# A RetNet attention block with an MLP behind it: how two token blocks start while weights arrive, and how two head pairs share the first batch

## The chip, the cores and the metric

One core of a Trainium2 chip. The metric is the device time of one execution in microseconds (us); the span is the time from the first to the last instruction in a profiled execution, about 2 to 3 us less. TensorE is called PE in the profile, VectorE DVE, ScalarE ACT, GpSimd POOL, SyncE SP.

## The reference, cut to what matters

```python
# q, k, v: (8 batches, 8 heads, 576 tokens, 64); float32
scores = (1/sqrt(64)) * q @ k^T
gamma  = 1 - 2**(-5 - h)                    # one per head
Dmat   = gamma**(i - j) where i >= j, else 0
attn   = (scores * Dmat) @ v
x      = attn as (4608 tokens, 512)
h      = x @ w_in                            # (512, 2048), float64 in memory
g      = max(h, 0) + alpha * min(h, 0)       # alpha: (2048,)
out    = g @ w_out                           # (2048, 512), float64 in memory
```

The weights and alpha are float64, so each 0.5 MB piece of weights is fetched raw and turned into float32 by three engines. The attention is done in chunks of 64 tokens: inside a chunk by scores, mask and values, between chunks by a running state, the scan. The 18 blocks of 256 tokens then go through the MLP. Most blocks use a scheme of seven products instead of eight, which needs sums and differences of weight blocks, the combinations.

## The kernel before: the parts concerned

The program works through 32 pairs of heads, four to a batch. Each pair runs transposes, scores, states with the scan, and values; between them stand units of the MLP and, at the start, weight pieces.

```python
def load_piece(src, dst):                       # one weight piece, 32 in all
    raw = raw_tile(at)
    nc.sync.dma_start(raw, src)
    lo, hi = raw[:, :, :, 0], raw[:, :, :, 1]
    nc.scalar.activation(a, hi.bitcast(FP32), ACTF.Abs)
    nc.scalar.activation(lo, lo.bitcast(UINT32), ACTF.Copy, scale=2.0 ** -29)
    nc.vector.tensor_scalar(a, a, HI_MIN, HI_MAX, ALU.max, ALU.min)        # the clamp
    c = ps_h.tile(...)                                                     # PSUM
    nc.vector.tensor_scalar(c, a.bitcast(INT32), 3, 0x3FFFFFF8, ...)       # the shift
    nc.vector.scalar_tensor_tensor(out=dst, in0=hi, scalar=-0x40000000, in1=c, ...)
    nc.gpsimd.tensor_tensor(out=dst, in0=dst, in1=lo, op=ALU.add)          # the last addition
# ... cut ...
def states(n, kn, vn):
    # ... 16 matmuls into ps ...
    nc.vector.tensor_copy(su[:, 0], ps[0][:, 0])
    for j in range(1, NJ - 1):                                             # the scan, 8 steps
        nc.vector.tensor_tensor(out=su[:, j], in0=ps[j % 2][:, j // 2], in1=su[:, j - 1], op=ALU.add)
    for h2 in range(2):
        nc.scalar.copy(sm[half(h2), :, h2], su[half(h2)])
# ... cut ...
for n, (b, c) in enumerate(pairs):
    if n + 1 < len(pairs):
        loaded[n + 1] = load_pair(n + 1)
    # ... cut ...
    kT, qT = transposes(n);            load_weights(2)
    at = scores(n, kT, qT);            load_weights(2)      # n < 8: four pieces a pair
    states(n, kn, vn)
    values(n, vn, qT, at)              # 18 matmuls with at, 16 with the running state
    # ... units of the MLP in between, cut ...
```

The profile counts two records for each of these float32 matmuls (32, 36 and 32 in its timelines), one for a transpose. All instructions stand in the in-order queue of their engine. Only block 0 uses plain products (eight), because its weights can't be combined before they have arrived.

## Time and profile before

| | before |
|---|---|
| time, median of 3 | 1097.5 us (1097.39 to 1097.9) |
| span of the profiled execution, mean granted TensorE clock | 1094.3 us, 0.978 |
| values of pairs 0, 1, 2, 3 end | 24.8, 38.4, 53.5, 68.5 us |
| TensorE without a pause from | 161.35 us |

The times of the values are read in TensorE's timeline: start plus duration of the last group of `pv<-qT,sums`, which follows the scan of the same pair. They are the milestones, since a batch's MLP units need the values of its four pairs.

```profile
22.16 2.61 PE L522 MATMUL pv<-qT,sums 128*64 128x64 f32 x32 [1.87 <-ACT sums L509]
36.18 2.17 PE L522 MATMUL pv<-qT,sums 128*64 128x64 f32 x32
51.35 2.17 PE L522 MATMUL pv<-qT,sums 128*64 128x64 f32 x32
66.34 2.17 PE L522 MATMUL pv<-qT,sums 128*64 128x64 f32 x32
```

Each pair follows the last by 14 to 15 us.

### The profile page before, as it was taken

The numbers are of one execution on the slowest core, as the hardware profiler recorded it, in microseconds if no ns is written. First come the engines' busy times: TensorE is split into PE (matmuls) and PEld (weight loads), VectorE is DVE, ScalarE is ACT, GpSimd is POOL, SyncE is SP. The second block draws the span as 40 slices with busy tenths as digits, with TensorE's granted clock in tenths as the row PEclk, the third lists the DMA queues.
The fourth block names the chain that finished last, engine by engine and source line by source line (L and its number), as shares of the span: only waits on it lengthen the run. The fifth ranks groups of instructions, "written<-read, shape, count | busy, mean of one in ns | idle before, by whom it ended". The sixth has DMA issues, their size and how long they took to land.

```text
span 1094.3 us, 25575 instructions
## 1 busy us (share of the span) xinstructions
PE 1052.2 (96%) x10465; PEld 940.9 (86%) x10465; DVE 777.3 (71%) x2160; ACT 162.8 (15%) x492; POOL 224.1 (20%) x264
## 2 busy tenths in 40 slices
PE   4769889999999999999999999999999999999998
PEld 3556668999999999999999999999999999999997
DVE  5577566776868776877676767687868676657665
ACT  3444431011001111101101111111111111000000
POOL 3888673110021102020012010210112000101000
PEclk9669999999999999999999999999999999999999
DMA  6746634121212222112121222222222010000000
GB/s 164 221 142 203 151 88 85 34 48 30 51 25 62 45 64 45 46 33 50 28 53 29 64 45 64 45 58 40 63 40 60 22 32 2 21 1 21 1 21 20
DMA packets 213205, 63.29 MB, mean 58 GB/s; under 512 B 202320, under 2 KB 202336, under 8 KB 213088
## 3 DMA queue, kind: packets, MB, share of 16 engines
q1 hardware_dynamic: 213088, 61.65, 23.9%
q8 instruction: 83, 1.36, 0.5%
q14 instruction: 34, 0.28, 0.1%
HBM read 52.17 MB, written 9.44 MB: 56 GB/s over the span
## 4 chain that ended last, share of the span: by engine, by line
PE 92%; DVE 3%; SPq 2%; ACT 1%; DMA 1%; issue 1%; POOL 0%; DVEq 0%; POOLq 0%; ACTq 0%
PE ph L376 40%; PE po L303 37%; PE pv L522 4%; PE ph L335 2%; PE pv L517 2%; PE ps L488 2%; PE po L318 2%; PE pu L500 2%; SPq L79 1%; DVE su L506 1%; SPq L81 1%; PE pt L461 1%; DVE wc L240 1%; DMA raw<-in_moe_w_in_dram 0%; DVE w_out L242 0%
## 5 line engine op out<-in xcount | busy, mean ns | idle before, releaser
L303 PE MATMUL po<-w_out,g 128*128 128x256 f32 x1904 | 433.3, 379 | 0.0
L303 PEld LDWEIGHTS po<-w_out,g 128*128 128x128 f32 x1904 | 351.4, 190 | 42.3 <-DVE osb L289 0.2
L387 DVE TENSOR_TENSOR g<-ph,g 128x256 f32<-128x256 f32 (+1 forms) x544 | 199.0, 386 | 201.3 <-PE ph L376 107.6
L376 PE MATMUL ph<-xb,w_in 128*128 128x128 f32 x2176 | 294.4, 278 | 0.0
L376 PEld LDWEIGHTS ph<-xb,w_in 128*128 128x128 f32 x2176 | 269.5, 192 | 9.0 <-issue 0.7
L376 PE MATMUL ph<-xt,w_in 128*128 128x128 f32 x1632 | 226.7, 275 | 0.0
L376 PEld LDWEIGHTS ph<-xt,w_in 128*128 128x128 f32 x1632 | 204.1, 192 | 0.0
L398 DVE TENSOR_TENSOR g<-g 128x128 f32<-128x128 f32 x544 | 148.1, 313 | 8.2
L382 ACT COPY g<-ph 128x128 f32<-128x128 f32 x136 | 36.1, 265 | 650.5 <-PE ph L376 650.5
L443 POOL TENSOR_TENSOR vn<-vn,tab 128x512 f32<-128x512 f32 x64 | 46.4, 740 | 353.6 <-DMA vn<-in_v_dram 299.0
L390 DVE TENSOR_SCALAR g<-g,alpha 128x256 f32<-128x256 f32 x272 | 100.9, 413 | 4.8
L392 DVE SCALAR_TENSOR_TENSOR g<-g 128x512 f32<-128x512 f32 x136 | 100.6, 740 | 4.1
L359 POOL TENSOR_TENSOR xt<-xb,xt 128x256 f32<-128x256 f32 x34 | 25.1, 738 | 186.3 <-ACT xb L432 185.9
L506 DVE TENSOR_TENSOR su<-pu,su 128x64 f32<-128x64 f32 x224 | 49.8, 222 | 9.3 <-PE pu L500 0.5
L509 ACT COPY sums<-su 64x512 f32<-64x512 f32 x64 | 39.4, 616 | 76.4 <-DVE su L506 75.6
L432 ACT COPY xb<-pv 128x128 f32<-128x128 f32 (+1 forms) x176 | 30.0, 269 | 123.9 <-PE pv L522 123.9
L522 PE MATMUL pv<-qT,sums 128*64 128x64 f32 x1024 | 43.2, 240 | 2.2 <-ACT sums L509 2.1
L335 PE MATMUL ph<-xb,w_in 128*128 128x256 f32 x128 | 38.1, 442 | 5.4 <-DVE g L343 3.1
L359 POOL TENSOR_TENSOR xt<-xb 128x256 f32<-128x256 f32 x17 | 12.6, 742 | 148.0 <-PE ph L376 147.9
L522 PEld LDWEIGHTS pv<-qT,sums 128*64 128x64 f32 x1024 | 38.1, 151 | 5.1 <-ACT sums L509 2.7
L517 PEld LDWEIGHTS pv<-at,vn 64*64 64x64 f32 x1152 | 24.6, 147 | 20.6 <-issue 18.9
L491 DVE TENSOR_TENSOR at<-ps,mask 128x320 f32<-128x320 f32 x64 | 28.5, 482 | 16.5 <-PE ps L488 16.5
(77 smaller groups left out, 619.1 us busy)
## 6 DMA issues: line engine op xcount, KB each, us to landing
out_dram<-osb SPq DMA_DIRECT2D x36, 256.0 KB, 2.1
kn<-in_k_dram SPq DMA_DIRECT2D x64, 128.0 KB, 2.7
vn<-in_v_dram SPq DMA_DIRECT2D x64, 128.0 KB, 2.6
kx<-in_k_dram SPq DMA_DIRECT2D x96, 72.0 KB, 2.6
qn<-in_q_dram SPq DMA_DIRECT2D x96, 72.0 KB, 2.6
raw<-in_moe_w_out_dram SPq DMA_DIRECT2D x12, 512.0 KB, 5.1
raw<-in_moe_w_in_dram SPq DMA_DIRECT2D x11, 512.0 KB, 5.4
w_in<-in_moe_w_in_dram SPq DMA_DIRECT2D x5, 512.0 KB, 5.4
```

Source lines behind the costliest of these rows:

```text
L303: nc.tensor.matmul(acc[kb][n // 2][:, n % 2, :], g[:, x, :], w_out[i][:, y, :], start=(i == 0 and n % 2 == 0), stop=(i == NU - 1 and (n % ...
L335: nc.tensor.matmul(ph[:, x], w_in[i // UST][:, cc // 2 * 2 + x, cc % 2, f0:f0 + P], xb[0][:, cc], start=(cc == 0), stop=(cc == NCC - 1))
L376: nc.tensor.matmul(ph[m][:, o], w_in[i // UST][:, l, cc, f0:f0 + P], r[:, cc], start=(n in (0, 3) and cc == 0), stop=(n in (2, 6) and cc = ...
L387: nc.vector.tensor_tensor(out=o, in0=x0, in1=x1, op=ALU.add)
L390: nc.vector.tensor_scalar(g[:, 4 + 2 * m:6 + 2 * m], g[:, 2 * m:2 * m + 2], 0.0, alpha[:, fc:fc + 1], ALU.min, ALU.mult)
L392: nc.vector.scalar_tensor_tensor(out=g[:, 0:4].rearrange("p x t -> p (x t)"), in0=g[:, 0:4].rearrange("p x t -> p (x t)"), scalar=0.0, in1 ...
L398: nc.vector.tensor_tensor(out=g[:, o, :], in0=g[:, x0, :], in1=g[:, x1, :], op=op)
L443: nc.gpsimd.tensor_tensor(out=t[0:rows, m], in0=t[0:rows, m], in1=tab[x][0:rows, c, m, :, None].to_broadcast([rows, n, 2, D]), op=ALU.mult)
L506: nc.vector.tensor_tensor(out=su[:, j], in0=ps[j % 2][:, j // 2], in1=su[:, j - 1], op=ALU.add)
L509: nc.scalar.copy(sm[half(h2), :, h2], su[half(h2)])
L517: nc.tensor.matmul(pv[p2][half(h2), m], vn[half(p2), m, h2], at[h2][half(p2), m], start=(m == 0), stop=False, skip_group_check=True)
L522: nc.tensor.matmul(pv[j % 2][half(h2), j // 2], sm[:, j - 1, h2], qT[:, chunk(j)], start=False, stop=(j >= NJ - 2), skip_group_check=True)
```

## The change

Its intent: make use of the first 160 us. Blocks 0 and 1 both run as plain products, all inside batch 1's pairs; pieces are fetched four ahead of their conversion and spread as 2,2,2,2,8,8,8,0 over the first eight pairs; the decay is kept local to a chunk, which needs smaller tables and puts a factor into the scan step and the mask; and pairs 1 and 3 get PSUM banks and SBUF tiles of their own, so that two pairs can be under way.

```diff
-    def load_piece(src, dst):
-        raw = raw_tile(at)
-        nc.sync.dma_start(raw, src)
+    AHEAD = 4
+    def fetch(n):
+        while npiece[0] < min(n, len(pieces)):
+            ...
+            nc.sync.dma_start(raw, src)
+            raws.append((raw, t))
+    def load_piece():
+        fetch(at + 1)
+        raw, t = raws.pop(0)
... (conversion unchanged)
-        if kb == 0:
+        if kb in PLAIN:                       # PLAIN = (0, 1)
-        combine(w_out[i], T_WORK)             # after each plain output
+        if kb == PLAIN[-1] and i % UST == UST - 1:
+            combine(w_in[i // UST], S_WORK)
+            for j in range(i + 1 - UST, i + 1):
+                combine(w_out[j], T_WORK)
+    ALT = (1, 3)
+    def ps_tile(n, x, shape, name):
+        if n in ALT:
+            return ps_o.tile(shape, FP32, tag=f"pso{n - 1 + x}", name=name)
+        return ps_a.tile(shape, FP32, tag="psa", name=name)
... (in states)
-            nc.vector.tensor_tensor(out=su[:, j], in0=ps[j % 2][:, j // 2], in1=su[:, j - 1], op=ALU.add)
+            nc.vector.scalar_tensor_tensor(
+                out=su[:, j], in0=su[:, j - 1], scalar=gch[:, c:c + 1],
+                in1=ps[j % 2][:, j // 2], op0=ALU.mult, op1=ALU.add)
... (in the loop over pairs)
+    PIECES = (2, 2, 2, 2, 8, 8, 8, 0)
+    UNITS = (0, 0, 0, 0, 4, 4, 4, 4)
+        parts = [(PIECES[n] + i) // 4 if early else 0 for i in range(4)]
         kT, qT = turned.pop(n) if n in turned else transposes(n)
+        load_weights(parts[3])
         at = scores(n, kT, qT)
+        load_weights(parts[2])
         states(n, kn, vn)
+        load_weights(parts[1])
         values(n, vn, qT, at)
+        load_weights(parts[0])
... (decay tables, nine loads a pair instead of twelve, alpha: cut)
```

## The prediction

> **What bounds the kernel now.** I read the page first, then the stretches of ten microseconds at its start, then TensorE's instructions in order of time, last the waits of the DMA queue. On the page, the strip of 40 slices (27.4 us each) shows where TensorE is not busy, and the chain that ended last says which engine carries the end.
>
> ```profile
> PE   4769889999999999999999999999999999999998
> PEclk9669999999999999999999999999999999999999
> PE 92%; DVE 3%; SPq 2%; ACT 1%; DMA 1%; issue 1%; POOL 0%; DVEq 0%; POOLq 0%; ACTq 0%
> ```
>
> The reader is to see that TensorE carries 92% of the chain and that all it loses lies in the first six slices, about 161 us. Busy time undercounts the loss there, because slices 2 and 3 also ran at a granted clock of 0.6. The stretches (columns: length, then busy time of PE, PEld, DVE, ACT and POOL, granted clock, DMA share, GB/s) show it closer:
>
> ```profile
> 20.00:30.00 10.00, 6.52 (x54) 4.78 (x47) 8.09 (x12) 7.80 (x18) 4.97 (x4) 1.00 0.81 228
> 30.00:40.00 10.00, 6.68 (x145) 6.08 (x145) 4.78 (x14) 4.50 (x12) 7.69 (x9) 0.66 0.87 270
> 40.00:50.00 10.00, 6.59 (x81) 4.51 (x80) 8.36 (x19) 3.95 (x10) 9.27 (x11) 0.50 0.81 250
> 60.00:70.00 10.00, 7.00 (x113) 6.08 (x108) 4.45 (x15) 2.97 (x10) 9.58 (x10) 0.50 0.66 201
> 70.00:80.00 10.00, 6.44 (x92) 4.89 (x90) 9.38 (x17) 5.35 (x11) 7.55 (x9) 0.84 0.18 41
> 120.00:130.00 10.00, 7.17 (x90) 5.18 (x88) 9.76 (x22) 3.08 (x6) 6.27 (x6) 0.94 0.64 84
> ```
>
> No engine is full in the first 70 us. Batch 0's four pairs run one after the other, each a chain over PE, ACT, DVE and POOL, with four weight pieces in the in-order queues of those engines. The values matmuls of pairs 0 to 3 start at 22.2, 36.2, 51.4 and 66.3 us, so a pair takes 15 us, for about 5 us of TensorE work at full clock. TensorE's own order gives the units of the sum (start, time to the end of the last, operation, count):
>
> ```profile
> 101.34 3.72 PE L335 MATMUL ph<-xb,w_in 128*128 128x256 f32 x16
> 104.89 3.60 PE L318 MATMUL po<-w_out,g 128*128 128x512 f32 x8
> ...
> 161.35 1.05 PE L376 MATMUL ph<-xb,w_in 128*128 128x128 f32 x8
> ...
> 936.07 3.19 PE L303 MATMUL po<-w_out,g 128*128 128x256 f32 x14
> 939.09 1.05 PE L376 MATMUL ph<-xb,w_in 128*128 128x128 f32 x8
> ```
>
> A plain unit (one 128-row slice of hidden width for 256 tokens) is 104.89 - 101.34 = 3.55 us in, plus about 3.5 us out: 7.05 us. A seven-product unit is 6.15 us, the step of its rows in the later trace (936.07 to 942.22). From 161.35 us on TensorE never stops.
>
> **What the Trainium skill says.** "TensorE: Matmul & The Clock Gate", Part 1, says that the array runs at half its clock after an idle window of about 3.4 us and gets the rest back by sustained work. The trace agrees: granted 0.50 where TensorE had gaps, and the 40 scores matmuls take 1.54 us at 58.8 us against 0.82 us at 73.8 us. "FP8 and Floating Point Precision", TensorE Precision Notes, says that true fp32 takes four passes: 256 columns x 4 / 2.4 GHz is 0.43 us, and the trace has 3.55 us for eight such matmuls, 0.44 each. So a plain product can't be had cheaper. "SBUF — State Buffer", SBUF: two separate sides, says that VectorE and GpSimd share a port pair as an exclusive lock. The clamp of a weight piece takes 0.42 us alone and up to 1.50 us beside GpSimd work, which agrees. "DMA: Bandwidth & Descriptors", Issuing engines are not separate DMA queues, says that issuing from a second engine saves only sequencer time; here issuing costs 0.5 to 0.6 us apiece, and the first weight transfer waits until 15.43 us behind 25 of them.
>
> **The change, part by part.**
> (1) Block 1 becomes plain: eight units at 7.05 instead of 6.15 us. Cost: 8 x 0.9 = 7 us of TensorE work, on the bounding engine. The combinations of the weights move behind both blocks; GpSimd then does 16 x 1.30 + 32 x 0.75 = 45 us of them later, off the path.
> (2) All 16 plain units now run inside batch 1's four pairs, where before six or seven did. Before, pair 8 was reached with ten units of blocks 0 and 1 still owed.
> (3) Pieces per pair go from 4 each to 2,2,2,2,8,8,8,0. Per piece the rows give ACT 0.68 + 0.67, DVE 0.42 + 0.69 + 0.68 (1.8 to 2.1), POOL 1.3 us. Batch 0 therefore loses half of its interference (about 4 us of DVE work per pair) and all combinations.
> (4) Pairs 1 and 3 have buffers of their own, so two chains overlap. The pair's data still has two buffers per tensor: pair 2's v cannot load before pair 0's values are done.
> (5) Loads: 9 issues instead of 12 per pair, and pair 0's three for q on ACT's queue. Before the first weight piece stand 16 issues on the SP queue instead of 25: about 10 us instead of 15.43.
> (6) Chunk-local decay: fewer small VectorE instructions at the start (some 2 us sooner), the scan step and the mask fused with a scale. A scan step costs 0.22 us and TensorE is the bound later, so nothing in the steady state.
>
> Now the end of batch 0. Pair 0: k lands at about 4 us; alpha, which heads PE's queue, at 7 us instead of 9.9; values end near 22 instead of 24.8. Pair 1 ends near 26. Pairs 2 and 3 load from about 21 and 26 us (9 issues of 0.6 us and 2.6 us to land), then run a chain of about 11 us (pair 1 took 27.25 to 38.4 us). They end near 36 and 41. DMA is a second bound: four pairs at 0.88 MB and twelve pieces at 0.52 MB are 9.8 MB, at some 250 GB/s 39 us after a slow start. I take 45 us as an estimate, where before it was 69.
>
> Then batch 1 on TensorE: 16 x 7.05 = 113 us, and four pairs at 0.73 x 2 + 0.75 + 0.62 + 1.8 plus about 0.6 for the switches, 5.3 us, make 21: 134 us. How full will it be? Between 80 and 120 us of before, I count 38 us of full-clock work in 40 (four units in, four out, two to three pairs) with VectorE 70% and POOL 88% busy. From 120 to 161 us only 31 in 41, with pieces queued in front of the activation and pair 8's loads late. In batch 1 of after, VectorE has 24 pieces (44 to 50), 16 activations of 0.48 x 2 + 0.68 (26) and four pairs at 3 (12), near 85 of 140 us; POOL near 90. That resembles the good stretch, and loads are ahead. I take 94%: 143 us. So the last plain unit ends at 45 + 143 = 188 us.
>
> What is left from there: before, from 161.35 to 1094.3 us is 933.0. It held one plain output (3.4) and eight seven-product units of block 1 (49.2) that after doesn't have, and lacked pair 8's scores and states (1.8). So 933.0 - 3.4 - 49.2 + 1.8 = 882.2 us. Sum: 188 + 882 = 1070 us of span; the measured times lie 3.2 above the span (1097.5 against 1094.3). **Predicted: 1073 us**, 2.2% less.
>
> **The rivals.** (A) *The wait moves into batch 1.* The plain units have a single PSUM bank for their input products, so the next unit can start only when VectorE has read the last; 24 pieces in its in-order queue may come between. For: at 152.76 us of before PE waits 2.60 us for exactly that. Against: 80 to 120 us was nearly full. At 85%, which is what before made of 80 to 161 us, batch 1 takes 158 us and the time is 1088. (B) *Batch 0 stays serial.* The load of pairs 2 and 3 waits for buffers: the queue of before shows where.
>
> ```profile
> SPq L79 <- PE pu L500: 14.7, 4, 5.7
> SPq L229 <- POOL w_out L244: 9.3, 3, 6.5
> SPq L79 <- PE pv L517: 7.0, 2, 3.8
> ```
>
> If pairs keep nearly 14 us each, batch 0 ends at 60 and the time is again 1088. Against: half the pieces, no combinations. (C) *It goes better.* Batch 0 ends at 40 and batch 1 is 97% full, 138 us: 178 + 882 + 3 = 1063. (D) *The extra work wins.* Only if both (A) and (B) hold in full is the last plain unit at 60 + 158 = 218, later than the break-even of 212, and the time some 1103.
>
> **Range and chances.** The 2% line, 1075.5 us, corresponds to the last plain unit at 190 us, two behind my estimate. Batch 0 may be off by 6 us and batch 1 by 8, mostly independently: about 10 together. So 1062 to 1086 holds it 8 times in 10. The chance of over 2% faster is 0.58, within 2% 0.41, slower 0.01.
>
> **What would show it.** Right: first matmul near 7 us, first weight issue near 10, pair 3's values done by 41 to 48 us, the last plain output at 180 to 196 us, granted clock 1.00 from about 50 us, later rows unchanged at 6.15 us a unit. TensorE's busy total falls only where it ran at half clock. Wrong: values of pairs 2 and 3 more than 10 us apart (B); idle time before plain input products put down to the activation on VectorE adding up to over 10 us (A); a gap of several microseconds at the first seven-product unit, waiting for combinations on GpSimd; or a slower steady state, which I count as excluded.

## More of the kernel before

The next lines are VectorE's part of pair 1 (start, duration, line, operation, count; in brackets what ended the idle time). The reader is to see that the scan's eight steps (the copy and seven additions) run together: 32.88 to 34.98 us.

```profile
31.30 0.89 DVE L491 TENSOR_TENSOR at<-ps,mask 128x320 f32<-128x320 f32 x2 [1.37 <-PE ps L488]
32.88 0.23 DVE L504 COPY su<-pu 128x64 f32<-128x64 f32 x1 [0.69 <-PE pu L500]
33.21 1.77 DVE L506 TENSOR_TENSOR su<-pu,su 128x64 f32<-128x64 f32 x7
```

## The result, and the profile after

| | before | after | predicted |
|---|---|---|---|
| time, median of 4 | 1097.45 us | 1088.27 us | 1073 |
| range | 1097.27 to 1097.9 | 1086.98 to 1088.38 | 1062 to 1086 |
| span, granted clock | 1094.3, 0.978 | 1085.2, 0.988 | 1070 |

The ratio is 0.9913, with a 95% interval of 0.9896 to 0.993: 0.9% less, within the 2%. A ratio is the mean time of one kernel's fast runs over that of the other's of the same rounds, so it is not quite the ratio of the medians. The time fell in the right direction, but by 9 us instead of 24.

The page of the changed kernel, in the same three lines as the prediction showed of before:

```profile
PE   4787999999999999999999999999999999999998
PEclk9889999999999999999999999999999999999999
PE 90%; DVE 4%; DMA 2%; issue 1%; POOL 1%; ACT 1%; SPq 0%; DVEq 0%; POOLq 0%; ACTq 0%
```

Slices 2 and 3 (27 to 81 us) ran at a granted 0.8 instead of 0.6, and slice 3 is at 8 instead of 6. From slice 5 on TensorE is full, where before two more slices showed an 8. But slice 4 (81 to 109 us) fell from 9 to 7, and in the chain VectorE has 4% where it had 3. The values of pairs 0 to 3:

```profile
25.53 2.17 PE L552 MATMUL pv<-qT,sums 128*64 128x64 f32 x32
...
39.89 0.69 PE L552 MATMUL pv<-qT,sums 128*64 128x64 f32 x4
40.93 1.62 PE L552 MATMUL pv<-qT,sums 128*64 128x64 f32 x28
...
47.61 1.16 PE L552 MATMUL pv<-qT,sums 128*64 128x64 f32 x32
...
59.75 1.98 PE L552 MATMUL pv<-qT,sums 128*64 128x64 f32 x32
```

They end at 27.7, 42.5, 48.8 and 61.7 us. Pairs 2 and 3 stand 13 us apart, so batch 0 gained 7 us over the 68.5 of before, where the prediction had 24. Here is the end of batch 1, where the last plain output runs, in TensorE's order:

```profile
199.82 0.81 PE L514 MATMUL ps<-qT,kT 64*64 64x64 f32 x40
200.56 1.16 PE L383 MATMUL ph<-xb,w_in 128*128 128x128 f32 x8
...
203.79 3.60 PE L323 MATMUL po<-w_out,g 128*128 128x512 f32 x8
207.22 1.05 PE L383 MATMUL ph<-xb,w_in 128*128 128x128 f32 x8
```

The last plain output ends at 207.22 us, and 3.97 us of later work (pair 8's scores and one seven-product input, 199.82 to 203.79) ran ahead of it. Without that it is 203.25. So the span divides as follows, beside the prediction's own terms:

| stage | predicted | measured | how |
|---|---|---|---|
| end of batch 0 | 45 | 61.73 | 59.75 + 1.98 |
| batch 1 on TensorE | 143 | 141.5 | 203.25 - 61.73 |
| the rest | 882.2 | 882.0 | 1085.2 - 203.25 |
| span | 1070 | 1085.2 | sum |

Two of three terms held to about 1%. All of the miss is batch 0.

**What happened in batch 0.** VectorE's timeline of pair 1, whose scan before ran together, now reads:

```profile
29.20 0.21 DVE L533 COPY su<-pu 128x64 f32<-128x64 f32 x1
29.34 0.68 DVE L244 SCALAR_TENSOR_TENSOR w_out<-raw,wc 128x512 int32<-128x512 int32 x1
29.93 0.27 DVE L535 SCALAR_TENSOR_TENSOR su<-su,gch,pu 128x64 f32<-128x64 f32 x1
...
36.12 0.55 DVE L518 SCALAR_TENSOR_TENSOR at<-ps,th,mask 128x320 f32<-128x320 f32 x1 [3.70 <-PE ps L514]
36.59 0.27 DVE L535 SCALAR_TENSOR_TENSOR su<-su,gch,pu 128x64 f32<-128x64 f32 x1
36.77 0.55 DVE L518 SCALAR_TENSOR_TENSOR at<-ps,th,mask 128x320 f32<-128x320 f32 x1
37.23 0.27 DVE L535 SCALAR_TENSOR_TENSOR su<-su,gch,pu 128x64 f32<-128x64 f32 x1
```

Steps of 0.27 us of the scan alternate with instructions of 0.68 us of a piece. Worse, pair 1's last two steps stand behind pair 2's mask, which waits 3.70 us for pair 2's scores. From first to last the scan takes 8.3 us (29.20 to 37.50), where before it took 2.1. Pair 1's values can't start before. The last of its matmuls that reads v ends at 39.48 us and frees the buffer into which pair 3's v is loaded, so in the queue of loads that v is issued only at 39.56 us. This is the first theory, called *scan*.

**What happened in batch 1.** It was as long as predicted, but it has one hole. The stretches of ten microseconds (length, PE, PEld, DVE, ACT, POOL, granted clock, DMA share, GB/s) and the three engines at the spot:

```profile
90.00:100.00 10.00, 8.61 (x73) 5.73 (x71) 9.90 (x8) 6.00 (x12) 9.92 (x10) 1.00 0.51 161
100.00:110.00 10.00, 3.96 (x10) 2.45 (x9) 9.85 (x18) 3.88 (x7) 7.67 (x9) 0.67 0.66 199
```

```profile
107.44 4.88 PE L344 MATMUL ph<-xb,w_in 128*128 128x256 f32 x15 [6.04 <-DVE g L350]
```

```profile
94.22 6.50 DVE L238 TENSOR_SCALAR wa<-wa 128x512 f32<-128x512 f32 x1
100.75 0.69 DVE L242 TENSOR_SCALAR wc<-wa 128x512 int32<-128x512 int32 x1
```

```profile
94.07 1.28 POOL L246 TENSOR_TENSOR w_in<-w_in,w_in 128x512 int32<-128x512 int32 x1
95.32 1.26 POOL L252 TENSOR_TENSOR w_in<-w_in 128x512 f32<-128x512 f32 x1
96.55 1.03 POOL L453 TENSOR_TENSOR vn<-vn,th 128x512 f32<-128x512 f32 x1
97.55 1.27 POOL L246 TENSOR_TENSOR w_in<-w_in 128x512 int32<-128x512 int32 x1
98.78 0.39 POOL L453 TENSOR_TENSOR vn<-vn,th 64x128 f32<-64x128 f32 x1
99.14 1.28 POOL L246 TENSOR_TENSOR w_out<-w_out,raw 128x512 int32<-128x512 int32 x1
100.50 0.80 POOL L252 TENSOR_TENSOR w_out<-w_out 128x256 f32<-128x256 f32 x1
```

One clamp, 0.41 us alone, took 6.50 us. It ended 0.3 us after GpSimd's first pause (100.42 to 100.50 us), behind six instructions of GpSimd on end. The activation that frees TensorE's only PSUM bank for input products stands behind it in VectorE's queue, with instructions of the pieces and a pair's masks between them (100.75 to 106.71 us), and TensorE stood for 6.04 us. "SBUF — State Buffer", section "SBUF: two separate sides", of the Trainium skill says that VectorE and GpSimd share a port pair as an exclusive lock and that "the other fully blocks". The trace agrees, and the block lasted through a whole run of GpSimd's instructions. This second theory is called *lock*.

### The profile page after: what moved, and what is told of

It reads as the page before. It is cut to its first block, busy times and chain, and to the rows that moved or that the text cites. A ratio compares the mean times of both kernels' runs of the same rounds, so it can differ in the third digit from the quotient of the medians.

```text
span 1085.2 us, 25041 instructions
## 1 busy us (share of the span) xinstructions
PE 1047.4 (97%) x10321; PEld 922.7 (85%) x10321; DVE 770.3 (71%) x2067; ACT 162.6 (15%) x485; POOL 222.1 (20%) x260
## 4 chain that ended last, share of the span: by engine, by line
PE 90%; DVE 4%; DMA 2%; issue 1%; POOL 1%; ACT 1%; SPq 0%; DVEq 0%; POOLq 0%; ACTq 0%
PE ph L383 38%; PE po L308 36%; PE ph L344 4%; PE po L323 3%; PE pv L552 3%; PE ps L514 2%; PE pv L547 2%; PE pu L529 2%; DVE wa L238 1%; DVE wc L242 1%; PE pt L485 1%; DMA w_in<-in_moe_w_in_dram 1%; DMA raw<-in_moe_w_in_dram 0%; DVE w_in L244 0%; POOL w_out L246 0%
## 5 line engine op out<-in xcount | busy, mean ns | idle before, releaser
L308 PE MATMUL po<-w_out,g 128*128 128x256 f32 x1792 | 407.8, 379 | 0.0
L383 PE MATMUL ph<-xb,w_in 128*128 128x128 f32 x2048 | 277.7, 279 | 0.0
L383 PEld LDWEIGHTS ph<-xb,w_in 128*128 128x128 f32 x2048 | 253.1, 192 | 8.2 <-DVE g L405 0.2
L383 PE MATMUL ph<-xt,w_in 128*128 128x128 f32 x1536 | 213.3, 275 | 0.0
L453 POOL TENSOR_TENSOR vn<-vn,th 128x512 f32<-128x512 f32 x64 | 45.3, 724 | 387.2 <-DMA vn<-in_v_dram 385.5
L344 PE MATMUL ph<-xb,w_in 128*128 128x256 f32 x256 | 63.0, 394 | 9.1 <-DVE g L350 9.1
L535 DVE SCALAR_TENSOR_TENSOR su<-su,gch,pu 128x64 f32<-128x64 f32 x224 | 62.5, 279 | 8.8 <-DVE su L533 0.5
L344 PEld LDWEIGHTS ph<-xb,w_in 128*128 128x128 f32 x256 | 47.8, 194 | 18.7 <-DVE g L350 10.3
L366 POOL TENSOR_TENSOR xt<-xb,xt 128x256 f32<-128x256 f32 x32 | 25.2, 788 | 174.9 <-ACT xb L442 174.3
L323 PE MATMUL po<-w_out,g 128*128 128x512 f32 x128 | 57.5, 592 | 0.0
L518 DVE SCALAR_TENSOR_TENSOR at<-ps,th,mask 128x320 f32<-128x320 f32 x64 | 32.2, 544 | 23.4 <-PE ps L514 23.4
L497 DVE STREAM_TRANSPOSE qT<-qn 128x576 f32<-128x576 f32 x24 | 18.7, 778 | 33.7 <-PE pv L552 33.7
```

What stands on the lines that cost most here:

```text
L308: nc.tensor.matmul(acc[kb][n // 2][:, n % 2, :], g[:, x, :], w_out[i][:, y, :], start=(i == 0 and n % 2 == 0), stop=(i == NU - 1 and (n % ...
L323: nc.tensor.matmul(acc[kb][m], g[:, 2 * x + m], w_out[i][:, 2 * x:2 * x + 2].rearrange("p x f -> p (x f)"), start=(i == 0 and x == 0), sto ...
L344: nc.tensor.matmul(ph[:, x], w_in[i // UST][:, cc // 2 * 2 + x, cc % 2, f0:f0 + P], xb[kb][:, cc], start=(cc == 0), stop=(cc == NCC - 1))
L383: nc.tensor.matmul(ph[m][:, o], w_in[i // UST][:, l, cc, f0:f0 + P], r[:, cc], start=(n in (0, 3) and cc == 0), stop=(n in (2, 6) and cc = ...
L453: nc.gpsimd.tensor_tensor(out=t[0:rows, m], in0=t[0:rows, m], in1=th[0:rows, x, None, 2 * c:2 * c + 2, None].to_broadcast([rows, n, 2, D]) ...
L535: nc.vector.scalar_tensor_tensor(out=su[:, j], in0=su[:, j - 1], scalar=gch[:, c:c + 1], in1=ps[j % 2][:, j // 2], op0=ALU.mult, op1=ALU.add)
```

## The experiments

Every experiment is an edit of the changed kernel, timed in three rounds (r11 and r12: up to five) beside the kernel before on the same chip; the chip is not the same for all runs, so kernels are compared by their ratios. `tc.issue_after(x)` puts the instructions inside it, in their engine's queue, behind instruction x; it sets an order and takes no wait away. The build orders each engine's queue itself, so the order in the source isn't always the order in the queue: in the changed kernel ten combinations ran in batch 0, though the source has them behind block 1.

Before the single runs, here is the table of all. "Pair 3" is the end of pair 3's values, "last plain" the start of the last plain output, "batch 1" their difference, "clamp" the longest of the clamps. A few kernels give a wrong result on purpose, as marked.

| run | edit | ratio to before [95%] | pair 3 | last plain | batch 1 | clamp |
|---|---|---|---|---|---|---|
| after | none | 0.9913 [0.9896, 0.993] | 61.7 | 203.79 | 142.1 | 6.50 |
| r1_late | combinations behind batch 0's scalings | 0.9962 [0.9946, 0.9978] | 58.2 | 208.54 | 150.4 | 10.90 |
| r2_noconv (wrong) | first 8 pieces not converted | 0.99 [0.9883, 0.9918] | 57.3 | 203.38 | 146.1 | 4.28 |
| r3_natv3 | third buffer for v | 0.9942 [0.9921, 0.9964] | 62.9 | 208.31 | 145.5 | 6.48 |
| r4_clamp | clamp writes PSUM | 0.985 [0.9832, 0.9869] | 57.7 | 198.18 | 140.5 | 0.70 |
| r5_order | transposes behind the values before them | 0.9935 [0.9906, 0.9964] | 62.3 | 208.35 | 146.0 | 1.55 |
| r6_clamplate | r4 + r1 | 0.9894 [0.9868, 0.992] | 55.8 | 200.35 | 144.5 | in PSUM |
| r7_clo | r4 + r1 + r5 | 0.9951 [0.9925, 0.9977] | 70.1 | 206.58 | 136.5 | in PSUM |
| r8_alt0 | one pair at a time | 1.003 [0.9999, 1.0061] | 75.0 | 216.29 | 141.3 | 2.93 |
| r9_scan | pieces behind the scan | 0.9853 [0.9828, 0.9878] | 53.0 | 196.75 | 143.8 | 2.96 |
| r10_bound (wrong) | r2 + r1 + pair 4 behind pair 3 | 0.9962 [0.9941, 0.9982] | 53.8 | 209.66 | 155.8 | 10.06 |
| r11_scanclamp | r9 + r4 | 0.9861 [0.9837, 0.9884] | 51.2 | 196.62 | 145.4 | in PSUM |
| r12_sca5 | r11, five pieces ahead | 0.99 [0.9879, 0.992] | 55.9 | 202.66 | 146.7 | in PSUM |
| r13_sa | r9, alpha by ScalarE | 0.9873 [0.9859, 0.9888] | 55.6 | 199.09 | 143.5 | 3.09 |
| r14_pipe | r9, next pair's scores earlier in the source | 0.989 [0.9867, 0.9912] | 54.9 | 200.20 | 145.3 | 2.95 |
| r15_pipea | r13 + r14 | 0.9869 [0.983, 0.9908] | 54.0 | 196.41 | 142.4 | 1.49 |
| r16_sl | r9 + r1 | 0.9939 [0.9925, 0.9954] | 53.7 | 206.17 | 152.5 | 5.83 |
| r17_bo (wrong) | r10 + order of pairs 2 and 3 enforced | 0.9924 [0.9898, 0.9951] | 51.5 | 204.93 | 153.5 | 10.91 |
| r18_real | r9 + that order + additions held | 0.9903 [0.9885, 0.9921] | 50.8 | 202.35 | 151.6 | 6.20 |

What is left behind the start of the last plain output is the same everywhere: span minus "last plain" is 881.4 to 881.5 us in the changed kernel and all 18 runs (1085.2 - 203.79, 1078.2 - 196.75, 1083.8 - 202.35). So a run's profiled span is decided by two numbers, the end of batch 0 and the length of batch 1, and nothing later has to be explained. Both numbers come from one profiled execution of each kernel, while the times of one kernel's executions lie up to 5 us apart in r9 (1078.88 to 1084.06) and nearly 9 in r15 (1078.32 to 1087.05). A difference of some 2 us between two kernels' milestones is therefore not clear of noise.

### The combinations in batch 0 (r1_late)

```diff
     def combine(w, work):
-        for o, x, y, op in work:
-            nc.gpsimd.tensor_tensor(out=w[:, o], in0=w[:, x], in1=w[:, y], op=op)
+        with tc.issue_after(last_scale[0].ins):     # last scaling of q or v emitted so far
+            for o, x, y, op in work:
+                nc.gpsimd.tensor_tensor(out=w[:, o], in0=w[:, x], in1=w[:, y], op=op)
```

> The changed kernel with one edit: GpSimd's combinations of the weights are held in issue order behind the scalings of q and v that precede them in the source; in the changed kernel ten of them had slipped in front, into batch 0 (30 to 48 us). Theory GpSimd queue: those ten (9.5 us of GpSimd) delay the scalings that pairs 2 and 3 wait for; then pair 3's values end near 53 us instead of 61.7, and the time falls by 6 to 9 us from 1088, to 1080 or so. Rival buffers (v of pairs 2 and 3 loads late because there are only two buffers): pair 3 ends within 2 us of 61.7 and the time within 3 us of 1088. Rival conversions (weight pieces in the in-order queues of ACT and VectorE): the same, within 3 us.

Measured: batch 0 ended 3.5 us sooner (58.2), and the time rose, to 1091.95 us. Held together, the combinations made longer runs on GpSimd: the longest clamp rose from 6.50 to 10.90 us, and TensorE's waits for the activation to 14.1 us in all, from 9.1. The combinations are a small part of the miss, and in their place they do less harm than together. These are the clamps of before, after and r1_late (count, then least, median and greatest duration in ns):

```profile
L236 DVE TENSOR_SCALAR wa<-wa x32: 413/562/1500, 21.1 to 150.6; 128x512 f32<-128x512 f32 x32
```

```profile
L238 DVE TENSOR_SCALAR wa<-wa x32: 410/432/6496, 18.9 to 126.0; 128x512 f32<-128x512 f32 x32
```

```profile
L238 DVE TENSOR_SCALAR wa<-wa x32: 408/421/10903, 18.4 to 130.0; 128x512 f32<-128x512 f32 x32
```

Before, no clamp passed 1.50 us. The median of after is lower; what stands out is the one longest.

### No conversion of the first eight pieces (r2_noconv)

```diff
         dst = pieces[at][1]
+        if at < 8:
+            nc.gpsimd.memset(dst, 0.0)      # wrong result on purpose
+            free.append(t)
+            return
```

> The changed kernel, wrong on purpose: the first eight weight pieces are still fetched but not converted (their place is filled with zeros once), so batch 0 has no piece on ACT or VectorE, and combinations remain. Theory conversions: the scan steps of pairs 0 to 2, which in the changed kernel alternate with pieces on VectorE (18.8 to 24.3 us for a scan of 2.2 us), run at once; pair 3's values end near 48 us and the time falls by 12 to 14 us, to about 1075. Theory GpSimd queue: part of that, since eight additions of 1.3 us go from GpSimd too: pair 3 near 53, about 1080. Rival buffers: pair 3 ends at 57 or later, 1084 or more.

Measured: pairs end at 25.2, 30.1, 42.1 and 57.3 us. Pair 1, whose scan had been cut up, gained 12 us, so the pieces were what held it. (Batch 0 was not free of pieces, as the expectation has it: the next two of them, not skipped, slipped into pair 3's scan, which took 4.1 us, 48.24 to 52.30.) But pairs 2 and 3 stayed 15 us apart: pair 3's values stood in TensorE's queue behind a transpose of pair 4's q that waited 4.82 us for its scaling on GpSimd. Where one hold-up goes, the order of the queue brings another.

### A third buffer for v (r3_natv3)

```diff
-        vn = nat.tile([P, NM, 2, D], FP32, tag="nat_v", name=f"vn_{n}")
+        vn = nat.tile([P, NM, 2, D], FP32, tag="nat_v", bufs=3, name=f"vn_{n}")
```

> The changed kernel with a third buffer for v alone (all that memory allows). Theory buffers: v of pair 3, issued at 39.56 us in the changed kernel after pair 1's values, is issued by about 30 us, and pair 3 ends 4 to 8 us sooner, near 55; the time falls to 1081 to 1084. Theories GpSimd queue and conversions: v arrives sooner but waits for its turn on GpSimd; pair 3 ends within 2 us of 61.7 and the time within 2 us of 1088.

Measured: pair 3's v is issued at 32.84 us, as was meant, and pair 3 ends at 62.9 us, no sooner. The late issue of v at 39.56 us is a result of pair 1's late values, and removing the wait for the buffer alone is worth nothing. Rival (B) of the prediction, as a matter of v's buffers, falls; as a matter of serial chains it doesn't. The buffers of k and q were not tried.

### The clamp out of SBUF (r4_clamp)

```diff
-        nc.vector.tensor_scalar(a, a, HI_MIN, HI_MAX, ALU.max, ALU.min)
         c = ps_h.tile([P, 2, HM], INT32, tag="psh1", name=f"wc_{at}")
-        nc.vector.tensor_scalar(c, a.bitcast(INT32), 3, 0x3FFFFFF8, ...)
+        nc.vector.tensor_scalar(c.bitcast(FP32), a, HI_MIN, HI_MAX, ALU.max, ALU.min)
+        nc.vector.tensor_scalar(c, c, 3, 0x3FFFFFF8, ...)
```

> The changed kernel with the clamp of a weight piece writing to PSUM instead of in place in SBUF (and the shift then working in place in PSUM); results the same. One clamp of the changed kernel took 6.50 us (94.22 to 100.72) while GpSimd ran five instructions on end. Theory port lock: with a PSUM output no clamp takes over 1 us and the idle time of TensorE near 100 us (6.0 us before an input product at 107.44, and slow work before it) shrinks by 6 to 9 us: about 1080. Rival load: VectorE is simply full between 80 and 125 us; the clamp costs some 0.25 us more in PSUM, 32 times, and the time is the same or up to 5 us longer.

Measured: 1079.65 us, ratio 0.985. Here is the clamp's line:

```profile
L239 DVE TENSOR_SCALAR wc<-wa x32: 682/694/696, 18.7 to 128.4; 128x512 f32<-128x512 f32 x32
```

Every clamp now takes 0.68 to 0.70 us: it is 0.28 us dearer alone, and none of the 32 was held up. "VectorE: DVE Perf Modes", section "Why PSUM operands drop a tier", says that any operand in PSUM keeps float32 at the slowest mode. Its reason is VectorE's one read port to PSUM, while here the output lies there; the trace agrees in the number, 0.69 against 0.41 us. So the lock on the clamp is shown: an edit of where the clamp writes (and of where the shift reads) ended it. TensorE's waits for the activation fell from 9.1 us in all to 1.5, and the hole at 100 us went. Another came at 111 to 116 us, where the pair's second half of the values waited 4.87 us for the scan's sums; so batch 1 gained only 1.6 us.

The last plain output came 5.6 us sooner (203.79 to 198.18), and most of this is batch 0 (4 us). That these 4 us are the lock's is not shown. The clamps of the changed kernel up to 61 us were held up by about 3 us in all, and the eleven of them cost 11 x 0.28 = 3.1 us more in PSUM (an estimate from the two traces). The edit also changed the order of GpSimd's queue: pair 2's q was scaled in one go from 29.81 us, where in the changed kernel a combination came before it and another in its middle, until 33.91 us.

### The order on TensorE (r5_order), and mixtures with it (r6_clamplate, r7_clo)

```diff
+        # last_pv: the last matmul of the values emitted so far
-        kT, qT = turned.pop(n) if n in turned else transposes(n)
+        with tc.issue_after(last_pv[0].ins) if 2 <= n <= 4 else ExitStack():
+            kT, qT = turned.pop(n) if n in turned else transposes(n)
```

> The changed kernel with one edit: on TensorE, the transposes of pairs 2, 3 and 4 are held in issue order behind the values of the pair before (pairs 0 and 1 may still overlap). In the changed kernel the next pair's transposes, scores and states stand in front of a pair's values and wait there for that pair's load and GpSimd scaling. Theory TensorE order: pair 1's values end near 31 us instead of 42.5, and pair 3's near 54 instead of 61.7; the time falls by 4 to 8 us if batch 1 does not change. Rival: a pair's own chain (load, scaling, scan) sets the pace, and holding back the next pair only takes overlap away: pair 3 ends at 61 us or later and the time is the same or longer. The hole near 100 us (one clamp of 6.5 us) is expected to stay.

Measured: pair 1 gained (36.1 instead of 42.5 us) and pair 3 didn't (62.3). TensorE stood 14.6 us in four waits for the scan, since nothing else was left ahead in its queue. That transposes of a later pair block the values is ruled out as the main cause. "TensorE: Matmul & The Clock Gate", Part 2, section "Step-by-step: what each phase is for", says that matmuls stay in program order; these waits agree: pair 2's transposes of k, which in the changed kernel ran at 28.56 us, stood behind the first of them until 36.00.

For r6_clamplate the edits of r4 and r1 are both made; for r7_clo those of r4, r1 and r5.

> The clamp in PSUM together with the combinations held behind the scalings. Holding the combinations alone made the hole of the clamp worse (one clamp of 10.9 us) and the time longer by some 5 us, though pair 3 ended 3.5 us sooner. Theory port lock: with no clamp on the shared port the lengthening cannot happen, no VectorE instruction before 130 us takes over 1.2 us, and the gain of batch 0 shows: 2 to 4 us less than the clamp alone, 1076 to 1078 on the scale where before is 1096. Rival: the longer time came from the combinations crowding GpSimd in batch 1, lock or not: then this run is slower than the clamp alone (1080).

> Clamp in PSUM, combinations held back, and TensorE's order held as well. If the three causes are separate, pair 3's values end near 50 us and the time is 5 to 8 us less than with clamp and combinations alone, near 1071, close to the predicted 1073. If they are the same wait seen from three sides (removing one uncovers the next), the gain over clamp and combinations is under 3 us.

Measured: r6 is slower than r4 (0.9894 against 0.985) but faster than r1 (0.9962), and its batch 1 is 5.8 us shorter than r1's (144.5 against 150.4). The pair r1 and r6 is a second piece of evidence for the lock: the same hold on GpSimd, with and without clamps that can be locked out. Over all kernels, though, the longest clamp does not set the length of batch 1: r5 (1.55 us) took 146.0 us and r11 and r12, with the clamp in PSUM, 145.4 and 146.7, all longer than the changed kernel with 6.50. Only the kernels in which work on GpSimd was held back and a clamp waited over 5.8 us stand out, with 150 to 156 us. In r7 the transposes held back make TensorE wait 19.6 us for the scan in batch 0, which ends at 70.1 us: these parts don't add up.

### One pair at a time (r8_alt0)

```diff
-    ALT = (1, 3)
+    ALT = ()
```

> The changed kernel without own buffers for pairs 1 and 3, so one pair of batch 0 at a time. If two pairs under way brought what the prediction gave it, pair 3 ends 8 us or more later (70 us) and the time is 8 us longer, near the kernel before. If instruction order had serialised the pairs anyway, pair 3 ends within 4 us of 61.7 and the time within 4 us.

Measured: batch 0 ends at 75.0 us, 13.3 us later than in the changed kernel, and the time is the same as before's or a little more (1.003). So the part "two pairs under way" did work: it is worth 13 us of batch 0 and, with the last plain output 12.5 us sooner, more than all of the gain. Without it the other parts of the change don't pay.

### The pieces behind the scan (r9_scan)

```diff
         for j in range(1, NJ - 1):
-            nc.vector.scalar_tensor_tensor(
+            last_su[0] = nc.vector.scalar_tensor_tensor(
...
+        if n < 4:
+            parts = [PIECES[n], 0, 0, 0]          # all of the pair's pieces at its end
...
-        load_weights(parts[0])
+        with tc.issue_after(last_su[0].ins) if n < 4 else ExitStack():
+            load_weights(parts[0])
```

> The changed kernel with one edit: VectorE's work on the two pieces of each of pairs 0 to 3 is held in issue order behind that pair's state scan. In the changed kernel the eight scan steps of a pair stood between piece instructions: from the first to the last step 5.5 us for pair 0, 8.3 for pair 1, 4.3 for pair 2, 4.7 for pair 3, against some 2.5 when they run together. Theory scan: values start about 3 us sooner in pairs 0 and 1 and 2 us in pairs 2 and 3; pair 3's values end near 54 us instead of 61.7 and the time falls by 4 to 8 us. Rival: what waits is the load and the scaling of the next pair, which stand in front of the values anyway; pair 3 ends within 2 us of 61.7, the time within 3 us.

Measured: 1080.57 us, ratio 0.9853. The scan of pair 2 runs in one, with a piece behind it:

```profile
36.69 0.23 DVE L535 COPY su<-pu 128x64 f32<-128x64 f32 x1 [1.14 <-PE pu L531]
37.02 2.18 DVE L537 SCALAR_TENSOR_TENSOR su<-su,gch,pu 128x64 f32<-128x64 f32 x7
39.11 0.76 DVE L238 TENSOR_SCALAR wa<-wa 128x512 f32<-128x512 f32 x2
```

Pairs 0 to 3 end at 25.0, 29.8, 42.6 and 52.95 us; pair 3's v is issued at 31.40 us instead of 39.56. This is 8.8 us of the 16.7 us that batch 0 was late, and the last plain output starts 7.0 us sooner. The scan theory is shown, as one half of the miss. The same number of pieces is converted, by the same instructions, in another order; the hold works on VectorE, but the pieces' place in the source moved for all engines, and what ScalarE's and GpSimd's part in this is was not separated.

### How low can batch 0 go? (r10_bound, r11_scanclamp, r12_sca5)

r10_bound is meant to take away what could be suspected at once: r2's conversions, r1's combinations, and pair 4's transposes go behind pair 3's values (r5's hold, for n == 4 alone). r11_scanclamp is r9 with r4's clamp; r12_sca5 also sets AHEAD = 5.

> Wrong on purpose (the first eight pieces are fetched, not converted), with the combinations held behind the scalings, and pair 4's transposes held behind pair 3's values on TensorE. It tells how much of the 16.7 us by which batch 0 missed the predicted 45 us is interference of these three together. If the predicted chain (pair 3 at 45 us) was right but for interference, pair 3's values end at 43 to 47 us. If loads and the chain itself were mis-sized, it ends at 50 us or later: the run without conversions alone had pair 3's scores at 45.2 us.

> Scan protected and clamp in PSUM. If the scan theory holds and is separate from the port lock, pair 3's values end near 51 us and the time is 3 to 6 us below the clamp alone (ratio 0.985 to before), that is a ratio near 0.981. If pieces held back in batch 0 only pile up in front of batch 1, the ratio stays at 0.985 or rises.

> As the run before, and raw pieces fetched five ahead instead of four. With the clamp in PSUM a new hole stood at 110 to 117 us, behind a piece that was asked for only when a raw buffer came free and landed 6.3 us later. If fetching ahead was what lacked, the hole shrinks and the time falls by 2 to 5 us against the run before. If the buffer's release, not the depth of fetching, sets the time of the request, nothing changes (within 1.5 us).

Measured: r10 ends pairs 2 and 3 at 40.4 and 53.8 us. The two stand 13.4 us apart. But pair 3 was not free of pieces: as in r2, the next two slipped between the steps of its scan, as VectorE's timeline shows.

```profile
46.42 0.21 DVE L540 COPY su<-pu 128x64 f32<-128x64 f32 x1
46.55 0.68 DVE L248 SCALAR_TENSOR_TENSOR w_in<-w_in,wc 128x512 int32<-128x512 int32 x1
...
49.26 1.22 DVE L542 SCALAR_TENSOR_TENSOR su<-su,gch,pu 128x64 f32<-128x64 f32 x4
```

This scan took 4.1 us (46.42 to 50.48) instead of 2.5, and TensorE waited 4.11 us for it. So r10 is no bound: without the two pieces pair 3 would have ended some 1.6 us sooner, near 52 us (an estimate from these lines), which is still not 45. r11 is no better than r9 or r4 alone (0.9861): pair 3 is 1.8 us sooner, and batch 1 is 1.6 us longer. r12, with one more piece ahead, ended batch 0 later (55.9) and is slower (0.99); why was not looked into. The hole that its expectation names is r4's; in r11 the longest wait of TensorE between 100 and 125 us is 2.03 us, so there was little left for r12 to shrink.

### The other 8 us: the start (r13_sa)

```diff
-    nc.vector.tensor_copy(alpha, aps)
+    nc.scalar.copy(alpha, aps)
```

(on top of r9)

> The scan-first kernel (pieces of each of the first four pairs held behind that pair's last scan step; it measured 0.985 of before, pair 3's values end at 52.95 us) with one more edit: alpha is copied out of PSUM by ScalarE, so that the decay chain on VectorE no longer stands behind it. In the scan-first kernel the chain stood still from 3.4 to 7.5 us and the first scaling of q on GpSimd began at 9.80 us. Theory start (the late tables delay every pair of batch 0 equally): first scaling near 7 us, values of pairs 0 to 3 each some 3 us sooner (25.0 to 22, 52.95 to 50), the time 2 to 3 us less (ratio 0.982). Rival (loads and the pair-to-pair chain set pairs 2 and 3): pair 0 ends 2 to 3 us sooner, pair 3 less than 1 us sooner, the time the same within 1 us.

Measured: the first scaling on GpSimd starts at 5.68 us instead of 9.80, and pair 0's values end at 23.8 instead of 25.0 us; pair 3's end at 55.6, no sooner. The rival holds: pairs 2 and 3 don't hang on the start. The alpha copy did stand ahead of the decay tables on VectorE, but it isn't part of the miss.

### The other 8 us: the serial order of pairs 2 and 3 (r14_pipe, r15_pipea)

```diff
+        if n < 3:
+            turned[n + 1] = transposes(n + 1)
+            ats[n + 1] = scores(n + 1, *turned[n + 1])
         values(n, vn, qT, at)
```

(on top of r9; r15 with r13's edit too)

> The scan-first kernel with transposes and scores of pairs 1, 2 and 3 put, in the program's order, ahead of the values of the pair before, so that the next pair's q and scores stand ahead of those values in TensorE's in-order queue. In the scan-first kernel pair 3's q was scaled at 38.9 us, but its transposes stood behind pair 2's values (42.49 us), and from there to the end of its values it took 10.4 us. Theory order (pairs 2 and 3 are serial because they are emitted serially): pairs 2 and 3 end 5 to 7 us apart instead of 10.4, pair 3's values end at 47 to 49 us, the time 4 us less (ratio 0.982 or lower). Rival (loads and GpSimd's queue set the pace: v of pair 3 is scaled only at 43.4 to 46.0 us): pair 3 ends at 52 to 54 us as before and pair 2 no sooner, or later since its values now wait behind pair 3's scores.

> Both edits together: transposes and scores of the next pair ahead of the values, and alpha copied by ScalarE. If both theories hold, pair 3's values end at 45 us or so, where the prediction had them, and the time is 6 us less than the scan-first kernel's, about 1075 (ratio 0.980). If neither holds, 52 to 54 us and a ratio of 0.985.

Measured: pair 3 at 54.9 and 54.0 us. For r14 this refutes nothing, since the edit did not do what it was to do. In its trace pair 2's values still stand ahead of pair 3's transposes of q, but for their last two matmuls:

```profile
41.20 1.97 PE L554 MATMUL pv<-qT,sums 128*64 128x64 f32 x30
43.09 0.66 PE L485 MATMUL pt<-ident,qn 128*128 128x128 f32 x4
43.68 0.33 PE L554 MATMUL pv<-qT,sums 128*64 128x64 f32 x2
```

The lesson is to look in the trace whether an edit took effect before reading its time.

### The other 8 us: GpSimd's queue (r16_sl)

r9's and r1's edits together.

> The scan-first kernel with the weight combinations on GpSimd held behind the last scaling of q and v of batch 0, so that in batch 0 GpSimd does only scalings and the last addition of each piece. Ten combinations (8.2 us of GpSimd) leave the stretch up to 53 us. Theory queue (GpSimd's in-order queue delays the scaling of v of pairs 2 and 3: pair 3's v at 43.4 us behind a piece and a combination): pair 3 ends 2 to 4 us sooner, at 49 to 51 us, but the combinations run together later, the longest clamp is over 6 us, and the time is no better than 0.985. Rival: pair 3 ends at 52 to 54 us all the same, and the time is worse than 0.985 by what the clamps wait.

Measured: pair 3 at 53.7 us, so the combinations ahead of v's scaling are not the cause. The time got worse by what the rival says: batch 1 takes 152.5 us, with a longest clamp of 5.83.

### The order enforced (r17_bo, r18_real)

```diff
+        if n == 2:
+            turned[3] = transposes(3)
+            ats[3] = scores(3, *turned[3])
+            sus[3] = states(3, loaded[3][0], loaded[3][3])    # the scan, without the copy into sums
-        values(n, vn, qT, at)
+        with tc.issue_after(last_ps[0].ins) if n == 2 else ExitStack():   # last matmul of states(3)
+            values(n, vn, qT, at)
```

(r17: on top of r10. r18: on top of r9, and each piece's last addition on GpSimd is held behind the scaling of the next pair's q and v.)

> Wrong result on purpose: the kernel of the lower bound (first eight pieces not converted, combinations late, pair 4's transposes behind pair 3's values; its values of pairs 2 and 3 ended at 40.4 and 53.8 us) with pair 3's transposes, scores, states and scan now held ahead of pair 2's values on TensorE. The earlier attempt at this by the program's order alone changed nothing: pair 2's values still stood ahead of pair 3's transposes of q. Theory emission (pairs 2 and 3 are serial because in TensorE's in-order queue all of pair 3 but part of k's transposes stands behind pair 2's values): pair 2 ends at 41 to 42 us, pair 3 at 45 to 47 us, 4 to 5 us apart instead of 13.4; that is the prediction's 45. Rival (v's load for pair 3, which waits for a buffer, or VectorE sets it): pair 3 ends at 50 us or later. The total time says nothing here, since late combinations cost what they cost in the lower-bound kernel.

> The same order in a kernel that computes the right result: the scan-first kernel with pair 3's transposes, scores, states and scan ahead of pair 2's values, and the last addition of each piece of pairs 0 to 2 on GpSimd held behind the scaling of the next pair's q and v. Theory emission plus GpSimd's queue: pair 3's v is scaled near 38 us instead of 43.4 to 46.0, its values end at 46 to 48 us instead of 52.95, and the last plain output starts 3 to 5 us sooner than in the scan-first kernel (196.75), the time 3 to 5 us less, ratio 0.981. Rival: batch 0 ends sooner but batch 1 gives it back (pieces later, longer runs on GpSimd that hold up the clamp): ratio 0.985 or worse with pair 3 at 46 to 48 us. Third: pair 3 no sooner than 52 us: the loads are the cause.

Measured in r17: pairs 2 and 3 end at 46.6 and 51.5 us. TensorE's order there, first pair 3's transposes of q, scores and states, then the values of pair 2 and of pair 3:

```profile
38.49 1.39 PE L492 MATMUL pt<-ident,qn 128*128 128x128 f32 x5 [3.66 <-POOL vn L460]
39.94 1.68 PE L521 MATMUL ps<-qT,kT 64*64 64x64 f32 x40
42.32 1.25 PE L537 MATMUL pu<-vn,kn 64*64 64x64 f32 x26 [0.70 <-issue]
...
44.67 1.97 PE L564 MATMUL pv<-qT,sums 128*64 128x64 f32 x32
...
49.73 1.75 PE L564 MATMUL pv<-qT,sums 128*64 128x64 f32 x32
```

The chains now overlap, 4.8 us apart as the theory said, but pair 2 pays for it: it ends 6.2 us later than in r10 and pair 3 only 2.4 us sooner. Pair 3's scan was again cut by two pieces (43.80 to 48.53, 4.7 us instead of 2.5). Besides, pair 3's v was ready late (its scaling began as it landed, at 37.44 us), and the chain ran slowly:

```profile
30.00:35.00 5.00, 3.87 (x84) 2.97 (x82) 1.80 (x6) 0.95 (x4) 0.00 (x0) 1.00 1.14 289
35.00:40.00 5.00, 1.45 (x7) 0.96 (x9) 1.40 (x5) 2.50 (x6) 2.78 (x4) 0.72 0.78 207
40.00:45.00 5.00, 4.30 (x114) 4.02 (x116) 2.21 (x6) 2.56 (x5) 0.00 (x0) 0.50 0.71 150
```

The DMA share is 1.14 from 30 to 35 us, the fullest of these stretches, and TensorE, which had little to do from 35 to 40, ran at a granted 0.50 after it. The serial order is so worth some 2 us: about as much as r13's edit, meant to help, moved pair 3 the other way (52.95 to 55.6), and no clear difference. The rival of the loads may have the rest on its side, and so may the cut scan and the half clock; no run here moved fewer bytes, so this is argued and not shown.

r18 is the same in a right kernel: pair 3 at 50.8 us, the earliest of all. Its scan ran whole (44.15 to 46.66 us), and its v was scaled from 37.75 to 39.14 us as the theory said, so neither pieces in the scan nor a late v is what it waits for. What the trace shows after that is a wait of TensorE of 2.06 us for ScalarE's copy of pair 3's qT, which stood behind the copy of pair 2's sums (38.60 to 39.86), and a granted clock of 0.50 from 40 to 45 us. And yet the time is 1086.07 us, since batch 1 took 151.6 us. One clamp again took 6.20 us (92.70 to 98.90), beside GpSimd instructions on end until 98.61 us; they are batch 1's own pieces, combinations and scalings, as in the changed kernel, and not the held additions. TensorE was busy only 4.64 us between 100 and 110 us.

## Why the prediction was wrong, point by point

- **The bound, TensorE's unit times, and the rest behind batch 1** were right: 882.0 against 882.2 us, no slower steady state, and no gap at the first seven-product unit (200.56 us starts as scores end). The prediction's 0.43 us for a product of 256 columns is an estimate from the clock that the page named just before it states; the eight products in its working are the sixteen records of its line.
- **"I take 94%: 143 us"** for batch 1 was right in size (141.5). Rival (A) came true in one spot only, for a reason that the prediction had seen but sized by the 1.50 us of before: a clamp locked out for 6.50 us. Outside that hole batch 1 was fuller than 94%: the 134 us of work counted in the prediction lay in 141.5 - 6.0 us. TensorE's waits for the activation were 9.1 us in all, just under the 10 us that the prediction named as (A)'s sign. So the good size is partly luck: a hole that was not counted on and a fuller rest cancelled, and the edits above moved batch 1 between 136.5 and 155.8 us.
- **The failed step is "I take 45 us as an estimate"** for the end of batch 0, with pairs 2 and 3 ending "near 36 and 41". They ended at 48.8 and 61.7. 16.7 us were lost there, more than the whole miss of the span, 15.2. The loads began about when the prediction had them (18.98 and 28.73 us, against 21 and 26). Mis-sized is the time from a pair's first load to its last value: 15 us for each pair in the prediction, 29.8 and 33.0 measured. What the runs put in its place: (1) The prediction took "half the pieces" for half the interference. What counts is where the pieces' instructions fall in VectorE's queue: with pieces, and in pair 1 also the next pair's mask, between its steps, a scan of 2.5 us took 4.2 to 8.3 us, and putting the same pieces behind the scan gave back 8.8 us (r9). (2) The prediction laid the two chains beside each other. With that order enforced pair 3 reached 51.5 (r17) and 50.8 us (r18), not 45; the order is worth some 2 us. (3) The last 6 us stay open. Candidates that the traces show side by side are the half clock after TensorE's pause and a wait for ScalarE (r18), and in r17 also loads that land late in a full DMA queue and a scan that was cut again; no run takes one of them away alone.
- **Rival (B)** had the right milestone, "Batch 0 ends at 60 and the time is again 1088": the run has 61.7 and 1088.27. Its cause was only half right: one more buffer for v changed nothing (r3), and two pairs under way did bring time (r8: without it 75.0 us).
- **Loads and the head of the program:** the first weight piece is issued at 10.91 us as predicted (near 10), the first matmul at 7.46 (near 7). But pair 0's values ended at 27.7 instead of near 22: besides the scan, the decay tables stood behind alpha's copy. r13 shows that this costs pair 0 1.3 us and the kernel nothing. The granted clock was 1.00 from 70 us on, the hole apart, and not from 50 (0.78 from 50 to 60, 0.88 from 60 to 70).
- **The 2% line** was set at a last plain unit at 190 us, "two behind my estimate". No right kernel here reached it; the best, r9, r11 and r15, start the last plain output at 196.4 to 196.8 us.

The best versions, r4 (0.985) and r9 (0.9853), beat both kernels, by 0.6% against the changed one (a quotient of the ratios). Their intervals overlap, and together they give no more (r11).

## What to carry to other kernels

Before halving interference in a stage that is a chain of waits, ask where in the in-order queue the remaining work falls: the same pieces cost 8.8 us between the short steps of a scan that they didn't cost behind it, and r10, meant as a bound without pieces, had two of them in its last scan. A milestone that comes sooner is worth only what the next stage can use, and holding back the combinations on GpSimd made longer runs, beside which a clamp took 5.8 to 10.9 us (r1, r10, r16, r17). Look in the trace whether an edit of the source's order reached the engine's queue, and whether what was to be taken away is gone.

## What the Trainium skill lacked or had wrong

- "SBUF — State Buffer", section "SBUF: two separate sides", says that whichever instruction starts first holds the shared pair "for the whole instruction". It doesn't say that the loser can stay out through a whole run of the winner's instructions. Here one clamp of 0.41 us waited through six GpSimd instructions on end and took 6.50 us, and up to 10.91 us in other orders (r17); in the changed kernel it ended 0.3 us after GpSimd's first pause in the profile, of 0.08 us, began.
- "SBUF — State Buffer", section "Who interferes with whom", says that an instruction of VectorE with at most one SBUF input outside the two-port modes does not contend with GpSimd. That was right: the clamp that writes PSUM took 0.68 to 0.70 us in all 32 cases. "VectorE: DVE Perf Modes", section "Why PSUM operands drop a tier", tells the slower mode only as a cap; that taking it on purpose can pay is on neither page. Here it cost 0.28 us a clamp, and the kernel with it was 0.6% faster (0.985 against 0.9913 of before's time), though how much of this is the lock's is not shown.
- No page that was read for this has the cost of interleaving two pieces of work in one in-order queue, which was the largest single effect shown here beside that of the two pairs under way: a scan of 2.5 us (36.69 to 39.20 in r9) stretched to 4.2 to 8.3 by pieces and, in the longest, a mask that waited 3.70 us; with the pieces behind the scan batch 0 ended 8.8 us sooner.
